# Five operand sums in three VectorE instructions, and score sums in other slots, in a fused attention and gated FFN kernel

## The chip, the cores and the metric

The kernel runs on one core of one Trainium2 chip. The metric is the device time of one execution in microseconds; lower is better. The kernel before took 802.4 us (median of three runs, 801.87 to 802.45).

## The reference

Cross-covariance attention over channels, then a gated feed-forward layer. Sizes: B = 4 batches, N = 6016 rows, C = 256 channels, 1536 hidden units.

```python
qn = q / (norm(q, axis=1) + 1e-6);  kn = k / (norm(k, axis=1) + 1e-6)
s = kn.transpose(0, 2, 1) @ qn / tau          # [B, 256, 256]
a = exp(s - max);  a /= a.sum(-1) + 1e-9
x = (v @ a).reshape(B * N, C)
out = (sigmoid(x @ w_gate) * (x @ w_val)) @ w_out
```

## The kernel before

Each batch has its attention matrix folded into the two FFN weights (`gh`), so that the main loop multiplies v directly with them. The main loop runs over 4 batches of 12 chunks; a chunk is four tiles of 128 rows (three in the last chunk of a batch). A chunk has 12 slots, one for each block of 128 hidden units. In slot f, `glu` makes the gate product (`ps_gate`, two matmuls of 512 columns) and the value product (`ps_val`, two more) on TensorE, ScalarE takes tanh of the first into `g_sb`, and VectorE multiplies (g_sb + 1) by `ps_val` into `hT[:, f]` (L682). The PSUM tiles `ps_gate` and `ps_val` have two buffers each, `g_sb` has three.

The output product of the chunk before (`out_work`, `product`) fills the slots: it is a Strassen-like scheme in which a 2 by 2 block product takes seven block products in place of eight. Its left operands are blocks of hT or sums of blocks (`sums`, made by `a_sum`, L704, on VectorE), its right operands are blocks of w_out or sums of them (`w_sums`, made once by `sum_w_out` on GpSimd, L228). A chunk's product is 84 matmuls of 128 columns, seven per slot. `part` and `whole` copy the results on ScalarE and add them on GpSimd (L759, L760, L775, L776), in float32 in SBUF.

The instructions of an engine run in the order in which the program writes them (a manual schedule). Slot by slot that is: `glu`; then an operand sum for the second half of the chunk before (`NEXT_SLOTS`); then the share of output matmuls (`run_work`); then an operand sum for the first half of this chunk (`OWN_SLOTS`); then the side work due in this slot (`side_work`). Side work prepares the next batch: it loads q and k, squares and accumulates them, makes the scores, and then the folded weights.

For the third and fourth batches the scores too are made in the seven-product form. The rows come in six groups of eight tiles, 16 slots apart; `s0` is the slot at which a group begins, counted from the start of the batch, and its place in a chunk is s0 % 12: 0, 4, 8, 0, 4, 8. `score_sums` makes sums of q and k blocks: number 0 at L351, number 2 at L359, numbers 3 and 4 at L364, all on VectorE; number 1 is made by DMA. `score_work` gives the score matmuls, which `queue_scores` puts in a queue and `run_scores` takes out evenly over the slots. `score_out` copies the two PSUM banks of scores at the end of the batch's scores, and `norms_mm` puts the norms into the second bank's free region.

All matmuls but the transposes at the start have the line L129, that of the helper `mm`.

Of the kernel before, what the change touches and what calls it, by code (L numbers as in the profile page):

```python
# [10 lines left out]
BF16 = mybir.dt.bfloat16  # L11
INT32 = mybir.dt.int32
ACT = mybir.ActivationFunctionType
ALU = mybir.AluOpType
PSUM = bass.MemoryType.PSUM


A_SUMS = (
    ((0, 1), ALU.subtract, (1, 1)),
    ((0, 0), ALU.add, (1, 1)),  # L20
    ((0, 0), ALU.add, (0, 1)),
    ((1, 0), ALU.add, (1, 1)),
    ((1, 0), ALU.subtract, (0, 0)),
)
B_SUMS = (
    ((1, 0), ALU.subtract, (0, 0)),
    ((0, 1), ALU.subtract, (1, 1)),
    ((1, 0), ALU.add, (1, 1)),
    ((0, 0), ALU.add, (1, 1)),
    ((0, 0), ALU.add, (0, 1)),  # L30
)

PRODUCTS = {
    "z1": (0, 1, 3),
    "y1": (1, (0, 0), 1),
    "x1": (2, (1, 1), 0),
    "x2": (2, 3, (0, 0)),
    "y2": (1, 2, (1, 1)),  # L40
    "z2": (0, 0, 2),
    "v2": (3, 4, 4),
}
ORDER = (
# [3 lines left out]
)  # L48
NEXT_SLOTS = {1: 1, 3: 3, 4: 2, 5: 0, 6: 4}
OWN_SLOTS = {7: 1, 8: 3, 9: 2, 10: 0, 11: 4}  # L50


@with_exitstack
def kernel(
# [20 lines left out]
    nc = tc.nc  # L75
    P = nc.NUM_PARTITIONS
# [9 lines left out]
    FC = DFF // P  # L86
# [3 lines left out]
    CH = TPC * P  # L90
# [73 lines left out]
    t0, nt = groups0[0]  # L164
# [39 lines left out]
    for f0, nf in pieces:  # L204
        if f0 + nf == DFF:
            load_v(0, 1)
        for w, src in enumerate((moe_w_gate, moe_w_val)):
            nc.gpsimd.dma_start(
                out=w_sb[w][f0 // FG][:, :, ds(f0 % FG, nf)],
# [3 lines left out]
    w_sums = consts.tile([P, len(B_SUMS), FC // 2, P], BF16)  # L213
    w_f32 = {}

    for n in range(FC // TPC):
        w_f32[n] = f32pool.tile([P, TPC, C], FP32, tag="f32", name="w_f32")
        nc.gpsimd.dma_start(
            out=w_f32[n], in_=moe_w_out.rearrange("(t p) c -> p t c", p=P)[:, n * TPC : (n + 1) * TPC, :]
# [5 lines left out]
    def sum_w_out(m, n):  # L225
        (k0, c0), op, (k1, c1) = B_SUMS[m]
        w = w_f32[n]
        nc.gpsimd.tensor_tensor(  # L228
            out=w_sums[:, m, n * 2 : (n + 1) * 2, :],
            in0=w[:, k0::2, ds(c0 * P, P)],  # L230
            in1=w[:, k1::2, ds(c1 * P, P)],
            op=op,
        )


    st = {}
# [454 lines left out]
    sums = {}  # L691

    def a_sum(b, ci, g, m):

        nt = groups[ci][1]
        half = nt // 2
        hT = hts[b, ci]
        if (b, ci, g) not in sums:
            sums[b, ci, g] = spool.tile(
                [P, len(A_SUMS), FC // 4, CH // 2], BF16, tag=f"s{g}", name="sums", bufs=2 - g  # L700
            )
        (r0, k0), op, (r1, k1) = A_SUMS[m]
        f0, f1 = g * (FC // 2), (g + 1) * (FC // 2)
        nc.vector.tensor_tensor(  # L704
            out=sums[b, ci, g][:, m, :, : half * P],
            in0=hT[:, f0 + k0 : f1 : 2, ds(r0 * half * P, half * P)],
            in1=hT[:, f0 + k1 : f1 : 2, ds(r1 * half * P, half * P)],
            op=op,
        )

    ffn = {}
    stores = []
# [91 lines left out]
    def run_work(work, share):  # L804

        upto = sum(w[0] for w in work) * share
        done = 0
        while work and done < upto:
            cost, fn, *args = work.pop(0)
            fn(*args)  # L810
            done += cost

    def store():
        while stores:
            b, ci = stores.pop(0)
            t0, nt = groups[ci]
            nc.sync.dma_start(out=out_rows[b][:, t0 : t0 + nt, :], in_=ffn.pop((b, ci))[:, :nt, :])
# [43 lines left out]
    for g, (t0, nt) in enumerate(groups0):  # L861
# [11 lines left out]
        while adds:  # L873
            w, last_sq = adds.pop()
# [55 lines left out]
    def side_work(b):  # L930


        side = {}

        def at(slot, fn, *a):
            side.setdefault(divmod(slot, FC), []).append((fn, a))

        for ci in range(NCH):
            nb, nci = (b, ci + 1) if ci + 1 < NCH else (b + 1, 0)
            lb, lci = (b, ci + 2) if ci + 2 < NCH else (b + 1, ci + 2 - NCH)  # L940
            if nb < B:
                at(ci * FC + 2, transpose_v, nb, nci)
            if lb < B:
                at(ci * FC + (10 if (b, ci) == (0, 0) else 0), load_v, lb, lci)
            if (b, ci) == (0, 0):
                for i in range(FC // TPC):
                    at(8, copy_w_out, i)
                for n, m in enumerate((1, 0, 3, 2, 4)):
                    for i in range(FC // TPC):
                        at(11 + 2 * n, sum_w_out, m, i)  # L950
        n = b + 1
        if n == B:
            return side
        first, last = (14 if b == 0 else 0), 8 * FC
        wide = [(t, min(2 * TPC, NT - t)) for t in range(0, NT, 2 * TPC)]
        at(first, acc_start, n)
        for g, (t0, nt) in enumerate(groups if b == 0 else []):
            s0 = first + g * (last - first) // NCH
            at(max(FC - 3, s0 - 12), load_qk, n, t0, nt)
            for u in range(nt):  # L960
                at(first + (t0 + u) * (last - first) // NT, score, n, t0, u)
            for w in range(2):
                at(s0 + 1 + 4 * w, narrow_square, n, g, w)
                slot = s0 + 3 + 4 * w
                at(slot + 2 if w == 0 and slot % FC == 8 else slot, narrow_add, n, g, w)
        step = (last - first) / len(wide)
        for g, (t0, nt) in enumerate(wide if b else []):
            s0 = first + int(g * step)
            halves = [(0, nt - TPC), (TPC, TPC)]
            if s0 >= 24:  # L970
                at(s0 - 24, load_qk, n, t0, nt)
            for i in range(4):
                at(s0 + 3 * i, acc_square, n, t0, 1 - i // 2, halves, i % 2)
            for w in range(2):
                at(s0 + 11 - 6 * w, acc_add, n, t0, w, halves)
            for m in (0, 2, 3, 4):
                at(s0 + 3 * max(0, m - 1), score_sums, n, t0, m, halves)
            ahead = 0 if g == 0 else 5
            at(s0 + 1 - ahead, score_sums, n, t0, 1, halves)
            at(s0 + 6 - ahead, score_sum_q, n, t0, halves)  # L980
            end = first + int((g + 1) * step) + 3
            at(s0 + 3, queue_scores, n, t0, halves)
            for slot in range(s0 + 3, end):
                at(slot, run_scores, s0 + 3, end, slot)
        if n + 1 < B:
            for g, (t0, nt) in enumerate(wide[:2]):
                at(NCH * FC - 24 + 16 * g, load_qk, n + 1, t0, nt)
        s0 = 8 * FC + 2
        if b == 0:
            at(s0, acc_fold, n, 0, (2, 1))  # L990
            at(s0 + 1, acc_fold, n, 1, (2, 1))
            at(s0 + 3, norms_mm, n)
            at(s0 + 4, root_seed, n)
            at(s0 + 4, root_steps, n)
            at(s0 + 10, norms_inv, n)
            at(s0 + 11, spread_both, n)
            at(s0 + 13, read_row, n)
        else:
            at(s0 - 3, acc_fold, n, 1, (4,))
            at(s0 - 2, acc_fold, n, 1, (2, 1))  # L1000
            at(s0, acc_fold, n, 0, (4,))
            at(s0 + 2, acc_fold, n, 0, (2, 1))
            at(s0 + 5, score_out, n, 0)
            at(s0 + 6, norms_mm, n)
            at(s0 + 7, score_out, n, 1)
            at(s0 + 7, root_seed, n)
            at(s0 + 7, root_steps, n)
            at(s0 + 12, norms_inv, n)
            at(s0 + 12, spread_both, n)
            at(s0 + 14, read_row, n)  # L1010
            at(s0 + 14, score_blocks, n)
        at(s0 + 22, scale_x, n, 0)
        at(s0 + 24, scale_x, n, 1)
        at(s0 + 25, exps, n, 0)
        at(s0 + 26, exps, n, 1)
        at(s0 + 28, all_sums, n)
        at(s0 + 28, gh_tiles, n)
        for i, piece in enumerate(gh_order):
            slot = s0 + 29 + 2 * i
            if slot < NCH * FC:  # L1020
                at(slot, gh, n, piece, *((pss, "s"), (psm, "m"))[i % 2])
            else:
                spill.setdefault((n, *divmod(slot - NCH * FC, FC)), []).append((gh, (n, piece, psm, "m")))
        return side
# [12 lines left out]
    for b in range(B):  # L1037
        side = side_work(b)
        for ci in range(NCH):
            final = (b, ci) == (B - 1, NCH - 1)  # L1040
            for f in range(FC):
                mid = gh_mid.get(f) if (b, ci) == (0, 0) else None
                glu(b, ci, f, None if mid is None else (lambda: gh_pieces(mid)))
                if prev is not None:
                    if f == 4:
                        store()
                    if f + final in NEXT_SLOTS and prev != (0, 0):
                        a_sum(*prev, 1, NEXT_SLOTS[f + final])
                    run_work(work, 1 / max(1, FC - final - f))
                if f in OWN_SLOTS and not final and (b, ci) != (0, 0):  # L1050
                    a_sum(b, ci, 0, OWN_SLOTS[f])
                for fn, a in spill.get((b, ci, f), []) + side.get((ci, f), []):
# [45 lines left out]
```

## Time and profile before

| engine | busy us of 799.6 | share |
|---|---|---|
| TensorE matmuls (PE) | 779.7 | 98% |
| VectorE (DVE) | 713.9 | 89% |
| ScalarE (ACT) | 525.6 | 66% |
| GpSimd (POOL) | 398.9 | 50% |

The span of the profiled execution, 799.6 us, is a little shorter than the time of a run. An instruction's busy time reaches from its start to its end as recorded, so where the next one starts before the end of the one before, single durations add up to more than the engine's time; the start of the next one is what shows the pace. In the rows of groups the columns are the line, engine, operation and tiles with shapes, the count, then busy time and mean ns of one, then the engine's idle time just before them and what ended it.

### The profile page before, as it was taken

To read this page: it belongs to the slowest core of one execution; us is meant where nothing else is said; L and a number is where in the kernel's file an instruction comes from. 1 tells how busy PE (TensorE), PEld (TensorE's weight loads), DVE (VectorE), ACT (ScalarE), POOL (GpSimd) and SP (SyncE) were. 2 spreads that over 40 slices of the span, in tenths; PEclk is the share of its full clock that TensorE was granted. 3 is DMA by queue.
4 is the path that set the end of the run, shared out by engine and by line. 5 is a ranking of instruction groups with operands and counts; after the bars stand their busy time and mean duration, and the time that the engine had idled before them with its cause. 6 is when DMAs were issued, how large, how long until landed. Compare 5 with 4: busy or idle time off the path is not lost.

```text
span 799.6 us, 18217 instructions
## 1 busy us (share of the span) xinstructions
PE 779.7 (98%) x6875; PEld 497.6 (62%) x6875; DVE 713.9 (89%) x1228; ACT 525.6 (66%) x891; POOL 398.9 (50%) x618
## 2 busy tenths in 40 slices
PE   3899999999999999999999999999999999999998
PEld 2556666666666666666666666666666566666666
DVE  5768999999979999999988999999998898998996
ACT  3666777766667767676667777666666565665664
POOL 3564545446453566565743565565744244444433
PEclk9999999999999999999999999999999999999999
DMA  9997758432777899862577699977234323423302
GB/s 214 198 199 133 131 96 139 93 67 54 135 143 140 170 174 200 171 114 54 115 137 146 132 163 186 174 147 139 56 66 84 67 56 80 74 60 72 82 27 74
DMA packets 82776, 95.16 MB, mean 119 GB/s; under 512 B 52512, under 2 KB 58528, under 8 KB 82688
## 3 DMA queue, kind: packets, MB, share of 16 engines
q0 software_dynamic: 25616, 55.85, 39.5%
q1 hardware_dynamic: 56496, 37.30, 21.2%
q8 instruction: 53, 0.87, 0.4%
q10 hardware_dynamic: 576, 0.85, 0.3%
q14 instruction: 35, 0.29, 0.1%
HBM read 79.04 MB, written 24.64 MB: 130 GB/s over the span
## 4 chain that ended last, share of the span: by engine, by line
PE 94%; DMA 4%; DVE 1%; issue 0%; ACT 0%; POOL 0%; DVEq 0%; POOLq 0%
PE ps_gate L129 30%; PE ps_val L129 30%; PE ps_o L129 27%; DMA qk_sb<-in_k_dram 4%; PE ps_s L129 4%; PE ps_gh L129 3%; DVE hT L682 0%; DVE sums L704 0%; DVE qs L364 0%; PE ps_end L129 0%; PE ps_n L129 0%; DVE x_sb L543 0%; PE ps_r L129 0%; ACT e_sb L561 0%; POOL qk_sb L148 0%
## 5 line engine op out<-in xcount | busy, mean ns | idle before, releaser
L681 ACT ACTIVATE g_sb<-ps_gate 128x512 f32<-128x512 f32 (+1 forms) x576 | 337.9, 589 | 224.7 <-PE ps_gate L129 212.3
L682 DVE SCALAR_TENSOR_TENSOR hT<-g_sb,ps_val 128x512 bf16<-128x512 f32 (+1 forms) x576 | 385.3, 670 | 67.1 <-ACT g_sb L681 52.3
L129 PE MATMUL ps_val<-vT,gh_H 128*128 128x512 bf16 (+1 forms) x1152 | 337.5, 375 | 0.5 <-DVE hT L682 0.5
L129 PE MATMUL ps_gate<-vT,gh_G 128*128 128x512 bf16 (+1 forms) x1152 | 337.6, 375 | 0.0
L704 DVE TENSOR_TENSOR sums<-hT 128x768 bf16<-128x768 bf16 (+1 forms) x460 | 283.4, 616 | 0.0
L129 PEld LDWEIGHTS <-sums 128*128 128x128 bf16 x2670 | 182.9, 98 | 82.2 <-DVE sums L704 0.4
L129 PEld LDWEIGHTS <-gh_H 128*128 128x128 bf16 x1152 | 112.7, 98 | 131.5 <-issue 1.2
L775 POOL TENSOR_TENSOR out_sb<-out_sb,m_sb 128x256 f32<-128x256 f32 x89 | 78.8, 885 | 186.1 <-ACT out_sb L765 163.0
L129 PE MATMUL ps_o<-w_sums,sums 128*128 128x128 bf16 x1602 | 154.4, 219 | 0.0
L129 PEld LDWEIGHTS <-hT 128*128 128x128 bf16 x1200 | 88.3, 98 | 46.8
L759 POOL TENSOR_TENSOR m_sb<-m_sb 128x128 f32<-128x128 f32 x89 | 44.9, 504 | 127.1 <-ACT m_sb L758 126.7
L129 PEld LDWEIGHTS <-gh_G 128*128 128x128 bf16 x1152 | 92.5, 98 | 12.2 <-DVE gh_G L629 0.3
L129 PE MATMUL ps_o<-w_out_sb,sums 128*128 128x128 bf16 x1068 | 96.2, 219 | 0.0
L129 PE MATMUL ps_o<-w_sums,hT 128*128 128x128 bf16 x1068 | 95.5, 219 | 0.0
L776 POOL TENSOR_TENSOR out_sb<-out_sb 128x256 f32<-128x256 f32 x89 | 76.6, 861 | 7.0
L760 POOL TENSOR_TENSOR m_sb<-m_sb 128x128 f32<-128x128 f32 x89 | 56.6, 636 | 7.0
L765 ACT COPY out_sb<-ps_o 128x512 f32<-128x512 f32 x89 | 52.2, 586 | 11.4 <-PE ps_o L129 8.9
L129 PE MATMUL ps_s<-qk_sb 128*128 128x256 bf16 (+1 forms) x194 | 34.1, 292 | 15.7 <-DMA qk_sb<-in_k_dram 8.6
L758 ACT COPY m_sb<-ps_o 128x384 f32<-128x384 f32 x89 | 42.6, 479 | 3.7 <-PE ps_o L129 1.1
L257 ACT ACTIVATE sq<-qk_sb 128x1024 bf16<-128x1024 bf16 (+3 forms) x36 | 35.6, 1009 | 12.0 <-DMA qk_sb<-in_k_dram 11.9
L297 ACT ACTIVATE sq<-qk_sb 128x1024 bf16<-128x1024 bf16 (+1 forms) x40 | 41.2, 1031 | 0.0
L129 PEld LDWEIGHTS <-qk_sb 128*128 128x128 bf16 x286 | 26.7, 102 | 21.7 <-issue 10.9
(102 smaller groups left out, 448.0 us busy)
## 6 DMA issues: line engine op xcount, KB each, us to landing
out_dram<-out_sb SPq DMA_DIRECT2D x43, 512.0 KB, 3.4
v_sb<-in_v_dram POOLq DMA_DIRECT2D x44, 256.0 KB, 5.4
acc<-sq POOLq DMA_DIRECT2D x16, 512.0 KB, 7.0
qk_sb<-in_q_dram POOLq DMA_DIRECT2D x14, 512.0 KB, 10.3
qk_sb<-in_k_dram POOLq DMA_DIRECT2D x14, 512.0 KB, 8.2
qs<-qk_sb POOLq DMA_DIRECT2D x20, 256.0 KB, 5.5
qk_sb<-in_q_dram POOLq DMA_DIRECT2D x15, 256.0 KB, 4.6
qk_sb<-in_k_dram POOLq DMA_DIRECT2D x15, 256.0 KB, 5.6
```

Source lines behind the costliest of these rows:

```text
L129: nc.tensor.matmul(out, lhsT=lhsT, rhs=rhs, start=start, stop=stop, **kw)
L257: nc.scalar.activation(out=sq[:, :nt, :], in_=src[:, :nt, :], func=ACT.Square)
L297: nc.scalar.activation(out=s["sq", w][:, u0 : u0 + n, :], in_=src[:, u0 : u0 + n, :], func=ACT.Square)
L681: nc.scalar.activation(out=g_sb[:, :n], in_=ps_gate[:, :n], func=ACT.Tanh, scale=0.5)
L682: nc.vector.scalar_tensor_tensor(out=hts[b, ci][:, f, :n], in0=g_sb[:, :n], scalar=1.0, in1=ps_val[:, :n], op0=ALU.add, op1=ALU.mult,)
L704: nc.vector.tensor_tensor(out=sums[b, ci, g][:, m, :, : half * P], in0=hT[:, f0 + k0 : f1 : 2, ds(r0 * half * P, half * P)], in1=hT[:, f0 ...
L758: nc.scalar.copy(m, states[p]["ps"][:, : 3 * P].rearrange("p (n c) -> p n c", c=P))
L759: nc.gpsimd.tensor_tensor(out=m[:, 1, :], in0=m[:, 1, :], in1=m[:, 2, :], op=ALU.add)
L760: nc.gpsimd.tensor_tensor(out=m[:, 2, :], in0=m[:, 1, :], in1=m[:, 0, :], op=ALU.add)
L765: nc.scalar.copy(o[:, p : p + half + 1 : half, :], states[p]["ps"].rearrange("p (t c) -> p t c", c=C),)
L775: add(out=ends, in0=ends, in1=states[p]["m"][:, 1:3, :], op=ALU.add)
L776: add(out=ends, in0=ends, in1=mids, op=ALU.subtract)
```

## The change

It does two things.

The first is on the operand sums of the output product. Five VectorE instructions for each half chunk, each of 768 elements per partition, become three: one of 768 and two that make two sums each, 1536 elements. For that the five sums are put in another order, and one of them, block (1, 0) minus block (0, 0), turns into its negative. To make up for it, one of the weight sums is multiplied by -1 once at the start. The product is the same sum of products. The sums, which were made in slots 7 to 11 and then 1, 3, 4, 5, 6, are now made in slots 7, 9, 11 and 1, 3, 5.

The second is on the score sums of the third and fourth batches. They are placed by a table (`SCORE_SLOTS`) that depends on where in a chunk the group begins, so that most fall into slots without operand sums; their products are queued five slots later (s0 + 8 in place of s0 + 3) and end five slots later; and the copies of the two score banks change places, the second bank first.

```diff
-A_SUMS = (
-    ((0, 1), ALU.subtract, (1, 1)),
-    ((0, 0), ALU.add, (1, 1)),
-    ((0, 0), ALU.add, (0, 1)),
-    ((1, 0), ALU.add, (1, 1)),
-    ((1, 0), ALU.subtract, (0, 0)),
-)
+A_STEPS = {0: (0, 1), 1: (1, 2), 2: (3, 2)}
...
-NEXT_SLOTS = {1: 1, 3: 3, 4: 2, 5: 0, 6: 4}
-OWN_SLOTS = {7: 1, 8: 3, 9: 2, 10: 0, 11: 4}
+NEXT_SLOTS = {1: 0, 3: 1, 5: 2}
+
+SCORE_SLOTS = {0: (0, 2, 12, 14), 4: (2, 8, 10, 13), 8: (4, 6, 9, 12)}
+OWN_SLOTS = {7: 0, 9: 1, 11: 2}
...
+        nc.gpsimd.tensor_tensor(out=out, in0=in0, in1=in1, op=op)
+        if m == 4:
+            nc.gpsimd.tensor_scalar(out=out, in0=out, scalar1=-1.0, scalar2=None, op0=ALU.mult)
...
-        (r0, k0), op, (r1, k1) = A_SUMS[m]
         f0, f1 = g * (FC // 2), (g + 1) * (FC // 2)
-        nc.vector.tensor_tensor(
-            out=sums[b, ci, g][:, m, :, : half * P],
-            in0=hT[:, f0 + k0 : f1 : 2, ds(r0 * half * P, half * P)],
-            in1=hT[:, f0 + k1 : f1 : 2, ds(r1 * half * P, half * P)],
-            op=op,
-        )
+        n = half * P
+        first, count = A_STEPS[m]
+        out = sums[b, ci, g][:, first : first + count, :, :n].rearrange("p m j n -> p j m n")
+        x = hT[:, f0:f1, : 2 * n].rearrange("p (j k) (r n) -> p j k r n", k=2, r=2)
+        if m == 0:
+            nc.vector.tensor_tensor(out=out[:, :, 0], in0=x[:, :, 0, 0], in1=x[:, :, 1, 1], op=ALU.add)
+        elif m == 1:
+            nc.vector.tensor_tensor(out=out, in0=x[:, :, 0], in1=x[:, :, 1], op=ALU.add)
+        else:
+            nc.vector.tensor_tensor(out=out, in0=x[:, :, :, 0], in1=x[:, :, :, 1], op=ALU.subtract)
...
-            for m in (0, 2, 3, 4):
-                at(s0 + 3 * max(0, m - 1), score_sums, n, t0, m, halves)
+            for m, slot in zip((0, 2, 3, 4), SCORE_SLOTS[s0 % FC]):
+                at(s0 + slot, score_sums, n, t0, m, halves)
...
-            end = first + int((g + 1) * step) + 3
-            at(s0 + 3, queue_scores, n, t0, halves)
-            for slot in range(s0 + 3, end):
-                at(slot, run_scores, s0 + 3, end, slot)
+            end = first + int((g + 1) * step) + 8
+            at(s0 + 8, queue_scores, n, t0, halves)
+            for slot in range(s0 + 8, end):
+                at(slot, run_scores, s0 + 8, end, slot)
...
-            at(s0 + 5, score_out, n, 0)
+            at(s0 + 5, score_out, n, 1)
             at(s0 + 6, norms_mm, n)
-            at(s0 + 7, score_out, n, 1)
+            at(s0 + 7, score_out, n, 0)
```

More of the change, by code (lines that the diff above doesn't have):

```diff
@@ L35 @@
 PRODUCTS = {
-    "z1": (0, 1, 3),
+    "z1": (0, 0, 3),
     "y1": (1, (0, 0), 1),
     "x1": (2, (1, 1), 0),
[L39 to L42, printed above, removed]
+    "x2": (2, 2, (0, 0)),
+    "y2": (1, 1, (1, 1)),
+    "z2": (0, 4, 2),
+    "v2": (3, 3, 4),
 }
@@ L227, in sum_w_out @@
         w = w_f32[n]
[L228 to L231, printed above, removed]
-            op=op,
-        )
+        out = w_sums[:, m, n * 2 : (n + 1) * 2, :]
+        in0, in1 = w[:, k0::2, ds(c0 * P, P)], w[:, k1::2, ds(c1 * P, P)]
+        nc.gpsimd.tensor_tensor(out=out, in0=in0, in1=in1, op=op)
+        if m == 4:
+            nc.gpsimd.tensor_scalar(out=out, in0=out, scalar1=-1.0, scalar2=None, op0=ALU.mult)
     st = {}
@@ L699, in a_sum @@
             sums[b, ci, g] = spool.tile(
-                [P, len(A_SUMS), FC // 4, CH // 2], BF16, tag=f"s{g}", name="sums", bufs=2 - g
+                [P, 5, FC // 4, CH // 2], BF16, tag=f"s{g}", name="sums", bufs=2 - g
             )
-        (r0, k0), op, (r1, k1) = A_SUMS[m]
         f0, f1 = g * (FC // 2), (g + 1) * (FC // 2)
-        nc.vector.tensor_tensor(
-            out=sums[b, ci, g][:, m, :, : half * P],
-            in0=hT[:, f0 + k0 : f1 : 2, ds(r0 * half * P, half * P)],
-            in1=hT[:, f0 + k1 : f1 : 2, ds(r1 * half * P, half * P)],
-            op=op,
-        )
+        n = half * P
[8 more added lines that the diff above has]
+            nc.vector.tensor_tensor(out=out, in0=x[:, :, :, 0], in1=x[:, :, :, 1], op=ALU.subtract)
     ffn = {}
```

## The prediction

> **What bounds the kernel now.** I read the page's head and its part 1 first, for the engine that is nearly always busy; then the chain that ended last, for whether that engine also sets the end; then the windows, for where it pauses; then the timeline, for what one pause is made of.
>
> ```profile
> span 799.6 us, 18217 instructions
> PE 779.7 (98%) x6875; PEld 497.6 (62%) x6875; DVE 713.9 (89%) x1228; ACT 525.6 (66%) x891; POOL 398.9 (50%) x618
> ...
> PE 94%; DMA 4%; DVE 1%; issue 0%; ACT 0%; POOL 0%; DVEq 0%; POOLq 0%
> ...
> L682 DVE SCALAR_TENSOR_TENSOR hT<-g_sb,ps_val 128x512 bf16<-128x512 f32 (+1 forms) x576 | 385.3, 670 | 67.1 <-ACT g_sb L681 52.3
> ...
> L704 DVE TENSOR_TENSOR sums<-hT 128x768 bf16<-128x768 bf16 (+1 forms) x460 | 283.4, 616 | 0.0
> ```
>
> TensorE is busy 779.7 of 799.6 us and carries 94% of the chain. VectorE is busy 89%, but only 1% of the chain is its own. The change works on VectorE (the L704 row and a few score sums). So what counts is how much TensorE waits for VectorE. The windows of 17 us say when TensorE pauses at all:
>
> ```profile
> 17.00:34.00 17.00, 11.56 (x95) 7.62 (x92) 13.93 (x24) 10.36 (x13) 7.48 (x13) 0.90 1.12 204
> 34.00:51.00 17.00, 16.27 (x94) 8.40 (x95) 12.92 (x24) 12.02 (x23) 9.03 (x13) 1.00 1.05 208
> 51.00:68.00 17.00, 17.00 (x108) 10.45 (x107) 10.63 (x18) 11.33 (x19) 15.30 (x24) 1.00 1.03 171
> ...
> 493.00:510.00 17.00, 16.66 (x158) 10.65 (x156) 15.89 (x25) 11.66 (x21) 12.55 (x19) 1.00 1.04 161
> 510.00:527.00 17.00, 16.79 (x160) 10.84 (x158) 16.75 (x28) 12.54 (x21) 8.69 (x13) 1.00 0.87 192
> ...
> 782.00:799.00 17.00, 14.75 (x165) 11.65 (x162) 9.83 (x20) 7.01 (x15) 6.00 (x10) 1.00 0.25 87
> ```
>
> The columns are the window, its length, then busy time of PE, weight loads, VectorE, ScalarE and GpSimd, and the granted clock. From 51 us to 782 us every window shows PE 17.00, but for two, which lack 0.34 and 0.21 us. The other idle time is the input phase up to 51 us and the last stores. The busy number hides short pauses, since the ends of matmuls are modelled; starts are safer. This is the timeline around the first pause:
>
> ```profile
> 498.51 0.59 PE L129 MATMUL ps_gate<-vT,gh_G 128*128 128x512 bf16 x2
> 498.94 0.59 PE L129 MATMUL ps_val<-vT,gh_H 128*128 128x512 bf16 x2
> 499.37 0.55 PE L129 MATMUL ps_o<-w_out_sb,sums 128*128 128x128 bf16 x7
> 499.76 0.28 PE L129 MATMUL ps_s<-qs 128*128 128x128 bf16 x2
> ...
> 501.24 0.59 PE L129 MATMUL ps_gate<-vT,gh_G 128*128 128x512 bf16 x2
> 502.09 0.59 PE L129 MATMUL ps_val<-vT,gh_H 128*128 128x512 bf16 x2 [0.25 <-DVE hT L682]
> ```
> ```profile
> 499.63 1.81 DVE L704 TENSOR_TENSOR sums<-hT 128x768 bf16<-128x768 bf16 x1
> 501.36 0.67 DVE L682 SCALAR_TENSOR_TENSOR hT<-g_sb,ps_val 128x512 bf16<-128x512 f32 x1
> ```
>
> Two 512-column matmuls start every 0.43 us, 0.215 each; seven 128-column ones take 0.39, 0.056 each. After 501.24 the next pair starts after 0.85 instead of 0.43: 0.42 lost. In the same way 0.25 is lost at 502.85 and 0.37 at 521.07 (a sum of q and k that took 1.85). These three, 1.04 us, with a few hundredths elsewhere, are all that TensorE loses to VectorE in the whole kernel: 1.1 us.
>
> **What the Trainium skill says.** "TensorE: Matmul & The Clock Gate", section "Wait — 56ns, not 53.3ns?", gives 55.6 and 215.7 ns from start to start for 128 and 512 columns on a warm array. The trace has 56 and 215, so TensorE is at its rate and only fewer matmuls, or fewer pauses, could shorten the middle. "VectorE: DVE Perf Modes", section "Mode 2×_1P", lets a two-input op take two elements a cycle where all operands are 16-bit with unit step. The trace agrees: 768 columns have a median of 550 ns and 1024 columns (L359, undisturbed) 682, thus 0.52 ns a column. "SBUF — State Buffer", section "SBUF: two separate sides", says that VectorE with two SBUF inputs and GpSimd exclude each other for a whole instruction. The trace agrees: the 1.81 us sum above lies over a GpSimd sum of 1.03 us.
>
> **The change, part by part.**
>
> 1. Matmuls: same number, shapes and operands per product; only the indices of the sums and a sign differ. Cost 0.
>
> 2. Five sums become three instructions. The elements stay at 5x768 per group. The old form is 550 ns, and 0.47 us from start to start in the timeline. The new pair of sums has 1536 columns: 550 + 768x0.52 = 950 ns, 0.87 from start to start. Per chunk (two groups): before 10x0.47 = 4.7, after 2x0.47 + 4x0.87 = 4.4 us. So about 0.3 us of a chunk of 16 us is freed, some 12 us in 46 chunks; as busy time, where the overlap of neighbours counts twice, 184x0.15 = 28 us, so L704's 283 become some 255 and VectorE's 714 some 687. Fewer instructions also meet fewer GpSimd sums. None of this is on the chain. Bounds for the new form, which no row shows: 0.95 us if rows of 256 contiguous values keep two elements a cycle (L359 reads rows of 128 in the same way and does), 1.65 us at one a cycle (768 more at 1.04 each, twice 0.52, would be added). I take 0.95.
>
> 3. Longer blocks. Behind each new sum the next hT waits, and behind that ps_val, which has two buffers. Slack: a slot without scores is 4x0.215 + 7x0.056 = 1.25 us, with them about 1.35. A free hT starts about 1.26 after its slot's first gate matmul (490.54 to 491.80) and ends 0.69 later, at 1.95; the ps_val that reuses its buffer starts at 2x1.35 + 0.43 = 3.13. Slack 1.2 us. A slot with hT (0.60) and a double sum (0.87) asks for 1.47, 0.12 over; the following slot has no sum and recovers that. A GpSimd wait of up to 1.26 (1.81 - 0.55) can just reach the slack.
>
> 4. Score sums (L351, L359, L364). They move mostly to even slots, where no operand sum is due. But of six groups per batch those that start at slot 4 or 8 of a chunk put one into slot 5: 0.60 + 0.87 + 0.60 = 2.07 in one slot, 0.72 late, which leaves 0.5 us. This occurs four times in the preparation of each of two batches. With a GpSimd wait of 1.26 each would stall 0.8 us, at most 6 us; with the usual small waits (616 mean against 550 median, 0.07) none. I take a fifth to a quarter of the eight at about 0.4 us: 0.8 us. Set against this, the crowded run of slots 7 to 11, where before each slot had a sum, is thinned out, and with it both pauses of the trace.
>
> 5. Score products start five slots later, all five inputs are ready a slot or more ahead, and the copies of the two banks change places: same matmuls in the same phase. The late end (slot 103) is before the first bank is copied at 105. Cost 0, hidden behind matmuls of the next chunks.
>
> 6. Three more GpSimd instructions turn the sign of one weight sum, once, near 65 us. The nearest row is L228, 764 ns for 256 columns: 2.3 us at most. Behind them only loads for later chunks and sums of m_sb wait, and the trace has GpSimd idle for 8.45 us before 74.77. Cost 0.
>
> Sum: 802.4 - 1.1 (pauses that go) + 0.8 (new ones) = 802.1; I say 802.0.
>
> **Rivals.**
>
> A, likeliest: paced by TensorE, 801.3 (all pauses gone) to 803.2 (some new ones). 80%.
>
> B, a new wait in place of the old: the double sums with a score sum or a GpSimd wait on top stall ps_val often. If all eight crowded slots cost 0.8 (6.4) and the old 1.1 goes, 802.4 + 5.3 = 807.7; if half do, 804.5. Slower. For it: both pauses in the trace are of this kind, and VectorE has few free slots. Against it: only three pauses in some 550 slots although sums of up to 1.85 occurred. 12%.
>
> C, the new access pattern loses the doubled rate: 4 double sums at 1.6 from start to start instead of 0.87, 2.9 us a chunk. VectorE would need 12x0.60 + 2x0.47 + 4x1.6 = 14.5 a chunk; with about 1 us of waits 15.5 against TensorE's 12x1.25 = 15.1, and in the 16 chunks with score sums (three each, 1.8) 17.3 against 16.2: 16x1.1 + 30x0.4 = 30 us, 832. Slower. Against it: L359 and L364. 3%.
>
> D, faster by more than the visible pauses: all that VectorE holds up in the trace is 1.1 us, so 800.5 would need gains in the input phase or at the end, where the change has nothing. 5%, for what a measurement may shift.
>
> **How the numbers follow.** The predicted time is A's, 802.0. The range is 801.0 to 804.2: below, all pauses gone and a little of spread (the three runs of before differ by 0.6); above, nearly to half of B. It leaves out the rest of B, C and most of D. 0.2% is 1.6 us: under 800.8 is D, 5%; over 804.0 is nearly all of B and C, 15%; the rest 80%.
>
> **What would show it.** The group of sums over hT has 276 instructions, the long ones near 950 ns, and VectorE's busy time falls by 20 to 35 us: step 2. A mean near 1.65 us would be C. The waits list has TensorE behind hT with under 1 us in all: steps 3 and 4; several us there, with ps_val after a slot 5 in windows from 200 to 560 us, would be B. Matmuls keep 0.056 and 0.215 us between starts: step 1. The prediction is wrong if TensorE pauses where it does not now, or if an unchanged stream of matmuls runs at another pace.

## The result, and the profile after

The changed kernel takes 804.94 us (median of six runs, 803.58 to 805.44); the kernel before, in six runs, 802.21 (801.67 to 803.05). The ratio is 1.0032, with a 95% interval of 1.0019 to 1.0045: slower, and above the range of 801.0 to 804.2. This is the direction of rival B. The execution with the profile took 805.34.

First the page of the changed kernel: span, part 1, the engines in the chain, and the rows of hT and of the operand sums, which are now L705 (the single sum), L707 and L709 (the double sums). Lines have moved by two or three: mm is L127, hT is L679.

```profile
span 803.6 us, 18036 instructions
PE 781.9 (97%) x6875; PEld 497.6 (62%) x6875; DVE 692.2 (86%) x1044; ACT 525.4 (65%) x891; POOL 437.7 (54%) x621
...
PE 93%; DMA 4%; DVE 2%; issue 1%; ACT 0%; POOL 0%; DVEq 0%; ACTq 0%; POOLq 0%
...
L679 DVE SCALAR_TENSOR_TENSOR hT<-g_sb,ps_val 128x512 bf16<-128x512 f32 (+1 forms) x576 | 382.9, 670 | 93.0 <-ACT g_sb L678 76.6
...
L707 DVE TENSOR_TENSOR sums<-hT 128x1536 bf16<-128x1536 bf16 (+1 forms) x92 | 103.7, 1127 | 0.0
...
L709 DVE TENSOR_TENSOR sums<-hT 128x1536 bf16<-128x1536 bf16 (+1 forms) x92 | 92.6, 1007 | 0.0
...
L705 DVE TENSOR_TENSOR sums<-hT 128x768 bf16<-128x768 bf16 (+1 forms) x92 | 50.7, 551 | 0.0
```

VectorE did what the change is for: 184 instructions fewer, and busy time down from 713.9 to 692.2 us. Yet its share of the chain rose from 1% to 2%, and the span by 4.0 us. GpSimd rose too, from 398.9 to 437.7, with three small instructions more: instructions of the same shape last longer, which I read as waiting that is recorded as part of their duration. Two of its rows (before: 885 and 636 ns):

```profile
L775 POOL TENSOR_TENSOR out_sb<-out_sb,m_sb 128x256 f32<-128x256 f32 x89 | 88.8, 998 | 174.9 <-ACT out_sb L765 153.5
...
L760 POOL TENSOR_TENSOR m_sb<-m_sb 128x128 f32<-128x128 f32 x89 | 78.0, 876 | 7.0
```

The windows of 17 us, in the columns of the prediction, say where TensorE now pauses. These are three of those with most of it. The list of waits has the wait of ps_val for hT as before, five times as long in sum; in its second line weight loads, which run ahead of the matmuls, wait for operand sums:

```profile
272.00:289.00 17.00, 16.22 (x154) 10.30 (x152) 15.05 (x21) 12.28 (x20) 9.61 (x15) 1.00 0.91 177
...
476.00:493.00 17.00, 15.94 (x151) 10.10 (x149) 16.38 (x24) 11.32 (x19) 12.98 (x16) 1.00 0.98 182
510.00:527.00 17.00, 16.66 (x159) 10.67 (x157) 15.81 (x21) 12.50 (x21) 11.07 (x14) 1.00 0.86 181
```
```profile
PE ps_val L127 <- DVE hT L679: 2.4, 5, 0.8
PEld L127 <- DVE sums L705: 1.9, 6, 0.4
```

All three lie where the scores of the third and fourth batches are made. By starts of matmuls, taking what each loses beyond its 0.056 or 0.216 us where that is over 0.06 us, TensorE pauses for 5.0 us between 45 and 790 us, against 1.1 us before. I call this sum "the pauses" below; records of matmuls that a trace lacks are left out of it. The difference of 3.9 us is the difference of the spans, 4.0. There are 18 pauses: in 16 of them, 4.7 us, ps_val waits for hT, and in two of 0.15 us a product waits for its double sum itself.

The largest pauses are two of 0.94 us, 194 us apart, at the same place of the two batches. The timeline of the changed kernel there, first TensorE, then VectorE, GpSimd and ScalarE:

```profile
282.47 0.59 PE L127 MATMUL ps_gate<-vT,gh_G 128*128 128x512 bf16 x2
283.84 0.59 PE L127 MATMUL ps_val<-vT,gh_H 128*128 128x512 bf16 x2 [0.78 <-DVE hT L679]
```
```profile
280.52 0.69 DVE L679 SCALAR_TENSOR_TENSOR hT<-g_sb,ps_val 128x512 bf16<-128x512 f32 x1 [0.65 <-ACT g_sb L678]
281.12 2.07 DVE L348 TENSOR_TENSOR qs<-qk_sb 128x1024 bf16<-128x1024 bf16 x1
283.11 0.67 DVE L679 SCALAR_TENSOR_TENSOR hT<-g_sb,ps_val 128x512 bf16<-128x512 f32 x1
```
```profile
280.99 0.88 POOL L366 DMA_DIRECT2D qs<-qk_sb  x1 [4.60 <-DMA qs<-qk_sb]
281.59 1.04 POOL L775 TENSOR_TENSOR out_sb<-out_sb,m_sb 128x256 f32<-128x256 f32 x1
282.71 1.06 POOL L776 TENSOR_TENSOR out_sb<-out_sb 128x256 f32<-128x256 f32 x1
```
```profile
278.94 1.06 ACT L294 ACTIVATE sq<-qk_sb 128x1024 bf16<-128x1024 bf16 x1
279.90 1.08 ACT L678 ACTIVATE g_sb<-ps_gate 128x512 f32<-128x512 f32 x2
```

The score sum of 0.68 us took 2.07. It started while GpSimd was issuing the accumulating DMA of `score_sum_q` (L366), with an output add (L775) queued behind. It ended 0.68 after 282.51, so it could not begin in earnest before the add was nearly over. hT came late by that, and ps_val had no free buffer.

The hold-up of 1.39 us is not all of it. The hT at 283.11 belongs to the slot whose gate matmuls start at 279.74; a free one would have come 1.26 us after that, at 281.00, so it was 2.1 us late, and less the slack of 1.2 us that is the pause of 0.94. The other 0.7 us come from the score sum's own 0.60 and from ScalarE: its square L294 stood in front of the tanh that the hT at 280.52 needed, and that hT was 0.9 us late. By this sum the hold-up with ScalarE on time would have cost next to nothing (0.60 + 0.60 + 1.39 of work in a slot of 1.37, so 1.2 late); that is an estimate, and no run tests it.

Behind a double sum no such help is needed. At 312.1 and 522.66 pauses of 0.45 and 0.27 us follow double sums that were held up in the same way, though the hT in front was on time. The first lies over the accumulating DMA of L305:

```profile
309.82 2.29 DVE L707 TENSOR_TENSOR sums<-hT 128x1536 bf16<-128x1536 bf16 x1
```
```profile
309.64 0.89 POOL L305 DMA_DIRECT2D acc<-sq  x1
310.25 1.04 POOL L775 TENSOR_TENSOR out_sb<-out_sb,m_sb 128x256 f32<-128x256 f32 x1
```

### The profile page after: what moved, and what is told of

Its sections match the earlier page's. It is cut to its first block, busy times and chain, and to the rows that moved or that the text cites. A ratio compares the mean times of both kernels' runs of the same rounds, so it can differ in the third digit from the quotient of the medians.

```text
span 803.6 us, 18036 instructions
## 1 busy us (share of the span) xinstructions
PE 781.9 (97%) x6875; PEld 497.6 (62%) x6875; DVE 692.2 (86%) x1044; ACT 525.4 (65%) x891; POOL 437.7 (54%) x621
## 4 chain that ended last, share of the span: by engine, by line
PE 93%; DMA 4%; DVE 2%; issue 1%; ACT 0%; POOL 0%; DVEq 0%; ACTq 0%; POOLq 0%
PE ps_val L127 30%; PE ps_gate L127 30%; PE ps_o L127 27%; DMA qk_sb<-in_k_dram 4%; PE ps_s L127 4%; PE ps_gh L127 3%; DVE hT L679 1%; DVE sums L707 0%; ACT g_sb L678 0%; PE ps_end L127 0%; ACT sq L294 0%; PE ps_n L127 0%; DVE acc L312 0%; DVE acc L331 0%; DVE x_sb L540 0%
## 5 line engine op out<-in xcount | busy, mean ns | idle before, releaser
L679 DVE SCALAR_TENSOR_TENSOR hT<-g_sb,ps_val 128x512 bf16<-128x512 f32 (+1 forms) x576 | 382.9, 670 | 93.0 <-ACT g_sb L678 76.6
L127 PE MATMUL ps_val<-vT,gh_H 128*128 128x512 bf16 (+1 forms) x1152 | 337.5, 375 | 2.5 <-DVE hT L679 2.4
L127 PE MATMUL ps_gate<-vT,gh_G 128*128 128x512 bf16 (+1 forms) x1152 | 337.6, 375 | 0.0
L127 PEld LDWEIGHTS <-sums 128*128 128x128 bf16 x2670 | 182.6, 98 | 82.8 <-DVE sums L705 1.9
L127 PEld LDWEIGHTS <-gh_H 128*128 128x128 bf16 x1152 | 112.6, 98 | 135.4 <-issue 6.6
L775 POOL TENSOR_TENSOR out_sb<-out_sb,m_sb 128x256 f32<-128x256 f32 x89 | 88.8, 998 | 174.9 <-ACT out_sb L765 153.5
L127 PE MATMUL ps_o<-w_sums,sums 128*128 128x128 bf16 x1602 | 154.7, 219 | 0.0
L127 PEld LDWEIGHTS <-hT 128*128 128x128 bf16 x1200 | 88.2, 98 | 46.9
L707 DVE TENSOR_TENSOR sums<-hT 128x1536 bf16<-128x1536 bf16 (+1 forms) x92 | 103.7, 1127 | 0.0
L759 POOL TENSOR_TENSOR m_sb<-m_sb 128x128 f32<-128x128 f32 x89 | 49.8, 559 | 97.9 <-ACT m_sb L758 97.4
L127 PEld LDWEIGHTS <-gh_G 128*128 128x128 bf16 x1152 | 92.8, 98 | 12.7 <-DVE gh_G L626 0.3
L127 PE MATMUL ps_o<-w_out_sb,sums 128*128 128x128 bf16 x1068 | 96.2, 219 | 0.0
L127 PE MATMUL ps_o<-w_sums,hT 128*128 128x128 bf16 x1068 | 95.5, 219 | 0.0
L709 DVE TENSOR_TENSOR sums<-hT 128x1536 bf16<-128x1536 bf16 (+1 forms) x92 | 92.6, 1007 | 0.0
L760 POOL TENSOR_TENSOR m_sb<-m_sb 128x128 f32<-128x128 f32 x89 | 78.0, 876 | 7.0
L776 POOL TENSOR_TENSOR out_sb<-out_sb 128x256 f32<-128x256 f32 x89 | 77.4, 870 | 7.0
L705 DVE TENSOR_TENSOR sums<-hT 128x768 bf16<-128x768 bf16 (+1 forms) x92 | 50.7, 551 | 0.0
L127 PE MATMUL ps_s<-qk_sb 128*128 128x256 bf16 (+1 forms) x194 | 34.9, 298 | 15.4 <-DMA qk_sb<-in_k_dram 8.8
```

The source lines that it names most:

```text
L127: nc.tensor.matmul(out, lhsT=lhsT, rhs=rhs, start=start, stop=stop, **kw)
L679: nc.vector.scalar_tensor_tensor(out=hts[b, ci][:, f, :n], in0=g_sb[:, :n], scalar=1.0, in1=ps_val[:, :n], op0=ALU.add, op1=ALU.mult,)
L705: nc.vector.tensor_tensor(out=out[:, :, 0], in0=x[:, :, 0, 0], in1=x[:, :, 1, 1], op=ALU.add)
L707: nc.vector.tensor_tensor(out=out, in0=x[:, :, 0], in1=x[:, :, 1], op=ALU.add)
L709: nc.vector.tensor_tensor(out=out, in0=x[:, :, :, 0], in1=x[:, :, :, 1], op=ALU.subtract)
L759: nc.gpsimd.tensor_tensor(out=m[:, 1, :], in0=m[:, 1, :], in1=m[:, 2, :], op=ALU.add)
```

## The experiments

Theory 1: a VectorE instruction with two SBUF inputs that meets a GpSimd add is held up, and double sums and moved score sums now overrun the slack of the PSUM buffers when that happens. Theory 2: the double sums are too long by themselves. Theory 3: the moved score sums are the cost, not the operand sums. All experiments were timed beside the kernel before. The times are medians of many executions; the pauses are those of one execution, the profiled one.

| kernel | us | before, same chip | ratio (95%) | pauses in its profile, us |
|---|---|---|---|---|
| changed | 804.94 | 802.21 | 1.0032 (1.0019-1.0045) | 5.0 |
| changed, again | 804.92 | 801.28 | 1.0045 (1.0032-1.0059) | 2.5 |
| sums only | 803.96 | 801.76 | 1.0022 (1.0013-1.0031) | 2.5 |
| scores only | 803.71 | 801.76 | 1.0026 (1.0018-1.0034) | 3.6 |
| no GpSimd adds | 801.23 | 801.76 | 0.9991 (0.9979-1.0004) | 0.9 |
| pairs split | 811.65 | 801.76 | 1.0116 (1.0101-1.0131) | 10.3 |
| sums in quiet slots | 802.37 | 801.64 | 1.0011 (1.0002-1.0020) | 2.1 |
| DMA later | 803.14 | 801.64 | 1.0034 (1.0018-1.0050) | 2.3 |
| DMA later, again | 802.43 | 801.28 | 1.0015 (1.0006-1.0024) | 1.9 |
| quiet and later | 802.57 | 801.64 | 1.0015 (0.9998-1.0032) | 1.7 |
| quiet start | 800.53 | 801.28 | 0.9996 (0.9985-1.0007) | 0.5 |
| quiet start, again | 800.65 | 801.50 | 0.9993 (0.9986-1.0000) | 0.6 |

**Sums only.** The score part goes back to what it was:

```diff
-            for m, slot in zip((0, 2, 3, 4), SCORE_SLOTS[s0 % FC]):
-                at(s0 + slot, score_sums, n, t0, m, halves)
+            for m in (0, 2, 3, 4):
+                at(s0 + 3 * max(0, m - 1), score_sums, n, t0, m, halves)
...
-            end = first + int((g + 1) * step) + 8
+            end = first + int((g + 1) * step) + 3
...
-            at(s0 + 5, score_out, n, 1)
+            at(s0 + 5, score_out, n, 0)
...
```

> The changed kernel with the score sums, score queue and score copies as before: the three-instruction operand sums alone. Theory 1 (a VectorE instruction of two SBUF inputs that meets a GpSimd add, and is twice as long, overruns the 1.2 us slack of the PSUM buffers): most of the new pauses stay, those behind L348 go; pauses of TensorE between 45 and 790 us of about 2 to 3.5 us in all, +1 to +2.5 us over before. Theory 3 (the moved score sums are the cost): pauses near 1 us, the time of before within 0.5 us.

2.2 us over before, pauses 2.5 us; the pauses of 0.94 us behind L348 are not there. Theory 3 falls as a whole explanation. But 1.5 of the 2.5 us are of another kind than the theories say: at 368, 371, 477, 483, 561 and 564 us a matmul starts right after the sum that it reads has ended (the largest, 0.48 us at 477, after an operand sum that took 1.81 us over L366 and L775). So late sums cost not only through hT and the PSUM buffers, but also directly.

**Scores only.** The kernel before, with SCORE_SLOTS, the later queue and the exchanged copies, but five operand sums in the old slots.

> The kernel before with the score part of the change alone: five operand sums in their old slots, score sums and score queue in the new ones. Theory 1: the two pauses of 0.94 us behind the score sum L348, which meets the issue of an accumulating DMA and the output add behind it, stay or move, the others do not exist: 1 to 3 us of pauses, 0 to +2 us over before. Theory 3: +2.5 us, the whole of the loss. If the moved slots only help: time of before or 1 us less.

2.0 us over before by the medians, at the upper end of what was expected. The pauses repeat in both batches: 0.4 us after the first score sum of a group had taken 1.52, 0.35 after another of 1.21, and 0.52 each in two crowds at the end of the scores, which also lie over GpSimd's adds. So each half costs about two parts in a thousand alone, and together they cost 0.32% and 0.45% in the two measurements. Within these intervals the two halves may simply add up, but they need not: the moved score sums were placed for slots that the new operand sums leave empty, and here the old ones still sit in slots 4, 6, 8 and 10.

**No GpSimd adds.** From the changed kernel, L759, L760, L775 and L776 are taken out; the block products are copied but not combined, so the output lacks these sums:

```diff
-            nc.gpsimd.tensor_tensor(out=m[:, 1, :], in0=m[:, 1, :], in1=m[:, 2, :], op=ALU.add)
-            nc.gpsimd.tensor_tensor(out=m[:, 2, :], in0=m[:, 1, :], in1=m[:, 0, :], op=ALU.add)
...
-            add(out=ends, in0=ends, in1=states[p]["m"][:, 1:3, :], op=ALU.add)
-            add(out=ends, in0=ends, in1=mids, op=ALU.subtract)
```

> The changed kernel without the four GpSimd adds that combine the block products (L759, L760, L775, L776 are left out, so the output lacks these sums); everything on the other engines is the same. Theory 1: double sums last 0.95 us without exception except against DMA issues, pauses fall from 5 us to under 1 us, about 801 us. Theory 2 (the double sums are too long by themselves, whatever GpSimd does): pauses stay near 4 to 5 us, 804 to 805 us.

This decides between theories 1 and 2. The double sums are as long and in the same slots, and the loss is gone. These are the double sums in that run:

```profile
L709 DVE TENSOR_TENSOR sums<-hT 128x1536 bf16<-128x1536 bf16 (+1 forms) x92 | 85.6, 931 | 0.0
L707 DVE TENSOR_TENSOR sums<-hT 128x1536 bf16<-128x1536 bf16 (+1 forms) x92 | 85.0, 924 | 0.0
```

1127 and 1007 ns became 924 and 931. What is left of the pauses, 0.9 us, is one event at 498 us; there hT waits 2.56 us for ScalarE, not for a sum. The work that was taken out also lay on GpSimd's own queue, so the run alone doesn't say that it is the meeting and not, say, a later DMA. The kernels with quiet slots below keep the adds and so speak to that.

**Pairs split.** The slots of the change, but two sums of 768 back to back for each double one:

```diff
-            nc.vector.tensor_tensor(out=out, in0=x[:, :, 0], in1=x[:, :, 1], op=ALU.add)
+            for r in range(2):
+                nc.vector.tensor_tensor(out=out[:, :, r], in0=x[:, :, 0, r], in1=x[:, :, 1, r], op=ALU.add)
...
```

> The changed kernel with each double sum written as two sums of 768, back to back in the same slot. Theory 1: the same elements block hT for the same time, and two instructions can be held twice, but GpSimd can come in between: pauses of 4 to 7 us, time within 1.5 us of the changed kernel. If the length of one instruction is what matters (GpSimd kept out for 0.95 us and then blocking for longer), pauses fall to 1 to 2 us and the time to within 1 us of before.

Worse than both expectations: 9.9 us over before, pauses of 10.3 us and 12 waits of ps_val for hT, 4.8 us in the list of waits. The timeline shows one such place, first VectorE, then GpSimd. Of the pair the first sum starts ahead of the add and takes 0.55 us; the second takes 1.08 over L777, and the next VectorE instruction, L331, 1.21 in place of 0.69 over L778:

```profile
136.32 1.55 DVE L711 TENSOR_TENSOR sums<-hT 128x768 bf16<-128x768 bf16 x2
137.80 1.21 DVE L331 TENSOR_TENSOR acc<-acc,sq 128x1024 bf16<-128x1024 bf16 x1
```
```profile
136.58 0.88 POOL L777 TENSOR_TENSOR out_sb<-out_sb,m_sb 128x256 f32<-128x256 f32 x1 [1.34 <-ACT out_sb L767]
137.53 0.92 POOL L778 TENSOR_TENSOR out_sb<-out_sb 128x256 f32<-128x256 f32 x1
```

Over the whole trace 197 of the 460 operand sums took over 0.1 us longer than alone, against 98 of 276 in the changed kernel, where they lie in the same slots, and 112 of 460 in the kernel before. So to make two sums in one instruction is worth having: in the same slots it is about 7 us better. That leaves the slots as what lost it.

**Sums in quiet slots.** To find these, take for each operand sum its duration less 550 ns (950 for a double one) and average by slot, the slot being that of the last hT in front of it. In the kernel before, slots 3, 5, 8, 9 and 11 have 0.23, 0.12, 0.19, 0.16 and 0.09 us of it; 1, 4, 6, 7 and 10 have 0.03 or less. In the changed kernel 3, 5, 9 and 11, just where the double sums went, have 0.23, 0.12, 0.17 and 0.06; 1 and 7, where the single ones went, 0.02 or less. The starts of GpSimd's adds lie in the same slots: L759 and L760 in 3 and 5, L775 and L776 in 8, 9, 11 and 0, since the products end there. With the sums-only kernel as its base:

```diff
-NEXT_SLOTS = {1: 0, 3: 1, 5: 2}
+NEXT_SLOTS = {1: 0, 2: 1, 4: 2}
...
-OWN_SLOTS = {7: 0, 9: 1, 11: 2}
+OWN_SLOTS = {6: 1, 7: 0, 10: 2}
```

> Three-instruction operand sums alone (as in the first experiment: score part as before), but in slots in which the trace of the changed kernel has hardly a GpSimd add: 1, 2, 4 and 6, 7, 10 in place of 1, 3, 5 and 7, 9, 11. If the meetings with GpSimd adds are the cost: mean of the double sums falls from 1.0 to 1.1 us to about 0.97, pauses from 2.5 to about 1 us or less, time about 802, 1.5 to 2 us under the first experiment. If the length of the double sums or the crowding of slots is the cost: 804, pauses of 2.5 us or more.

802.37, 0.7 us over before where the sums-only kernel was 2.2 over. The two ratios were measured on different chips and their intervals overlap, so by the times alone the gain isn't shown. What is shown is that the sums are no longer held up: the double sums come down to 943 and 948 ns, from 1125 and 992 in the sums-only kernel. The pauses remain at 2.1 us, more than expected. The largest, 0.85 us, follows a meeting of a double sum (1.67 us) and a score sum (1.21) with GpSimd; two of 0.32 us, at the start of both batches, follow none.

**DMA later.** The changed kernel with the accumulating DMA of q at slot s0 + 8:

```diff
-            at(s0 + 6 - ahead, score_sum_q, n, t0, halves)
+            at(s0 + 8, score_sum_q, n, t0, halves)
```

> The changed kernel with one edit: the accumulating DMA for the q sum (score_sum_q) is issued at slot s0+8 of its group in place of s0+1, so that GpSimd does not sit waiting for the copy in front of it while output adds queue up behind. If the worst waits (2.1 to 2.3 us for an instruction of 0.68 or 0.95) come from a VectorE instruction that starts during such an issue with an add queued behind: the two pauses of 0.94 us and that of 0.27 go, pauses fall from 5.0 to about 3 us, time 1 to 2.5 us less than the changed kernel. If the issue of the DMA has no part in it: same pauses at other places, time within 0.5 us of the changed kernel.

> The accumulating DMA for the q sum at s0+8, once more, since its interval was wide. If the pauses carry the time: 2.3 us of pauses against some 5 of the changed kernel, so 2 to 3 us less than it on the same chip. If the time does not follow the pauses: within 0.5 us of it.

The three pauses behind L366 are gone in both profiles, and the pauses are 2.3 and 1.9 us. The first timing showed no gain: its ratio is that of the changed kernel, with a wide interval, since four of its 22 executions took 808.7 to 811.0 us, for which no trace gives a cause. Its profiled execution also started the main loop 1.9 us later than that of the changed kernel (the matmuls that come at 48.1 us there come at 50.0), in the input phase, where the edit does nothing. The second timing, on one chip with the changed kernel, has 802.43 against 804.92, with intervals that don't overlap. The run of the unedited changed kernel beside it:

> The changed kernel, unedited, once more, so that it stands beside the next two on one chip. Pauses of 4 to 6 us at the same places of the two batches (the first slots of the fourth chunk of a batch, 0.9 us each), ratio to before 1.002 to 1.0045. If the pauses fall elsewhere from run to run, no place of the program but chance makes them.

Its two pauses of 0.94 us did not come back: in this profile another score group was hit, at 330 us, with 0.44 and 0.25 us behind a double sum of 2.27 us that met L366 and L775. Pauses of 0.10 to 0.22 us did return at 110, 176, 273, 355, 466 and 548 us, each behind a double sum that met m_sb's adds. That profiled execution took 802.8 us, the least of its six. L366 and L775 lay over the score sum L348 here too, at 281 us, but it started 0.07 us after the issue in place of 0.13, and took its usual 0.69 us. So which group is hit differs from run to run, by a few hundredths of a microsecond at this place; L366 waits for another DMA to land (4.60 us in the lines above), so its start isn't fixed by the program. The meetings with the adds of m_sb came back at the same places.

**Quiet and later**, with score sums placed in the slots that double sums leave free:

```diff
-SCORE_SLOTS = {0: (0, 2, 12, 14), 4: (2, 8, 10, 13), 8: (4, 6, 9, 12)}
+SCORE_SLOTS = {0: (3, 5, 9, 12), 4: (1, 4, 5, 8), 8: (0, 3, 7, 9)}
```

> The changed kernel with both edits, and its score sums placed so that they do not share slots with the double sums in 1, 2, 4, 6, 7, 10 (in slots 0, 3, 5, 8, 9, 11 of a chunk). If GpSimd meetings are the cause of all of the loss: pauses under 1.1 us, time equal to before or up to 1 us less, 801 to 802. If something else in the change costs: 803 or more.

802.57, within its interval of before but not under it. Of the 1.7 us of pauses 1.4 are 0.44 and 0.27 us at the start of the scores of both batches, with no GpSimd add near. There is only a crowd on VectorE, in slots where TensorE has no score matmuls yet and so is faster:

```profile
239.42 0.55 DVE L709 TENSOR_TENSOR sums<-hT 128x768 bf16<-128x768 bf16 x1
239.89 0.68 DVE L679 SCALAR_TENSOR_TENSOR hT<-g_sb,ps_val 128x512 bf16<-128x512 f32 x1
240.49 0.75 DVE L626 TENSOR_SCALAR gh_H<-ps_gh,rrow 128x512 bf16<-128x512 f32 x1
241.15 0.68 DVE L356 TENSOR_TENSOR qs<-qk_sb 128x1024 bf16<-128x1024 bf16 x1
241.75 0.68 DVE L679 SCALAR_TENSOR_TENSOR hT<-g_sb,ps_val 128x512 bf16<-128x512 f32 x1
242.35 0.95 DVE L707 TENSOR_TENSOR sums<-hT 128x1536 bf16<-128x1536 bf16 x1
```

VectorE works here without a gap from 238.82 us on, and hT comes 1.86 us after the one in front of it (239.89 to 241.75), where TensorE takes 1.14 us for a slot. So length and crowding do count, at this one place; theory 2 is not nothing.

**Quiet start.** The same, with the first group's score sums moved off that crowd:

```diff
-            for m, slot in zip((0, 2, 3, 4), SCORE_SLOTS[s0 % FC]):
+            for m, slot in zip((0, 2, 3, 4), SCORE_SLOTS[s0 % FC] if g else (3, 9, 12, 13)):
```

> The version with quiet slots and the later DMA, with the score sums of a batch's first group at slots 3, 9, 12, 13 in place of 3, 5, 9, 12. If the pauses of 0.44 and 0.27 us at the start of both batches came from the crowd of hT, folded-weight stores, score sums and double sums there and not from GpSimd: they go, pauses of about 0.3 to 0.6 us in all, time 0.5 us under before at best. If not: 1.7 us as they were.

> The last version once more, since its interval (0.9985 to 1.0007) leaves open whether it is faster than before. By the pauses (0.5 us against 1.1) it can be 0.6 us faster, a ratio of 0.9993; by the medians of the last run 0.75 us. If the ratio comes out at 0.999 to 1.000 again, it equals before or is a little faster; if above 1.001, the last run was luck.

Of these pauses 0.1 us is left in each batch. The page of the second run shows what the merged sums bring when hardly anything meets them (before: 713.9 us and 398.9 us):

```profile
span 798.9 us, 18038 instructions
...
PE 779.9 (98%) x6875; PEld 497.9 (62%) x6875; DVE 665.8 (83%) x1044; ACT 525.4 (66%) x891; POOL 379.0 (47%) x621
```

The medians are 0.75 and 0.85 us under before, ratios 0.9996 and 0.9993. The first interval holds 1, the second ends at it. The version beats the changed kernel by 4.4 us on one chip (800.53 against 804.92), with all GpSimd adds in place. That, with the run without adds, is what shows the meetings with GpSimd as the main cause; how much of the 4.4 us is due to the quiet slots, to the later DMA and to the moved score sums isn't separated. Over the kernel before it is ahead by about what the pauses had room for (1.1 less 0.5), and no more can be claimed.

## Why the prediction was wrong

Its frame held. TensorE sets the pace, the matmuls kept their 0.056 and 0.215 us between starts, and nearly all that the change did to the time it did through pauses of ps_val behind hT. Step 1 was right. Step 2 was right in the unit: an undisturbed double sum takes 0.95 us, so rival C was rightly set aside (its bound of 1.65 us should be 1.75 by its own terms, 950 and 768 times 1.04 ns). VectorE's busy time fell by 22 us, within the 20 to 35 us that the prediction gave, but not for its reason: on the page an overlap of neighbours counts once, so the 28 us don't apply. By step 2's 0.3 us a chunk some 12 us come from the shorter work, and the rest fits what the operand sums lost by being held up, which fell from 36 to 28 us. Step 3's slack of 1.2 us is confirmed by the largest pause: 2.1 us late, 0.94 lost. Steps 5 and 6 showed nothing.

One reading was wrong too. Of the three pauses of before, that at 502.85 isn't "in the same way": there the next matmul, a score product, starts at 503.16, right after the score sum that it reads has ended (502.43 and 0.68). Sums can hold TensorE directly, as they do in the sums-only kernel.

The step that failed is the count of new pauses. "I take a fifth to a quarter of the eight at about 0.4 us: 0.8 us", from step 4, stood for all new pauses; step 3 put those outside the eight crowded slots at nothing. The profile has 18 pauses, 5.0 us together. The eight slots, where a double sum and a score sum share slot 5, were not far off: seven of them paused, 1.3 us in all. The other 3.8 us came where the prediction had nothing: 1.9 behind the score sum L348, 1.1 behind double sums in slots 9 and 11 that met a DMA issue with an add behind it, 0.8 in six small ones. Three things were wrong.

- Step 4 took slots without operand sums to be free, and looked for danger only where three VectorE instructions fall into one slot. The two worst pauses came behind a score sum with no operand sum in its slot. What mattered there was GpSimd's work in the slot, and a late ScalarE in front of it.
- Step 4 used the usual wait (0.07 us on average over all sums) although the old sums were spread over ten slots of a chunk, five of them quiet. The change put all four double sums of a chunk into 3, 5, 9 and 11, where before a sum lost 0.23, 0.12, 0.16 and 0.09 us, and none into a quiet one. The trace of before held these numbers.
- Step 3 gave the double sum 1.26 us of wait at worst and found that this "can just reach the slack". By its own numbers it passes it: the wait and the 0.12 us by which the slot is over make 1.38, against 1.2. Waits of 1.34 us (2.29 less 0.95) occurred.

The sentence "Fewer instructions also meet fewer GpSimd sums" was true: 98 held-up sums in place of 112, and 28 us lost in place of 36. Yet TensorE paused more. What counts is not the sum of the waits but whether one of them, on top of a longer instruction, passes the slack. The pauses of before were expected to go, and they did go at 501 and 521 us; others came elsewhere. Rival B named the mechanism and was given 12%. That its 804.5 is near the 804.94 measured is luck: it took half of the eight slots at 0.8 us, and the eight cost 1.3 us in all. Its argument against, that only three pauses existed in some 550 slots, counted a layout that the change was about to leave.

## What to carry to other kernels

Where one engine sets the pace and another stands behind it with a slack of about one slot, average busy time says little; tabulate by slot how much longer than alone an instruction takes, and put the long ones into the slots where that is near zero. Merging two instructions with two SBUF inputs into one halved the number held up by GpSimd here (98 against 197), and splitting them back cost 7 us, but the merged one should lie where GpSimd has little to do. A DMA issued by GpSimd that has to wait for another transfer lets its other work pile up behind it (L366 waited eight times in the changed kernel, 30.2 us in all); issue it when its input has long landed, if its result has time.

## What the runs showed of the hardware

A DMA issue on GpSimd does not by itself hold up a VectorE sum, with few exceptions. In the kernel before, 67 such sums started during an issue with no GpSimd add before their end, and none was longer by more than 0.01 us; in the changed kernel one of 44 was, by 0.35 us (at 313.23), which is not explained. But where an add came directly behind the issue, 7 of 12 in the changed kernel were held up. Five of them lost 0.94 to 1.39 us, that is until shortly before the end of the add, although by the record the add had not started when they did; the other two started together with the add and lost 0.3 us. A VectorE sum that started ahead of an add with no issue under way was not delayed: 46 in the changed kernel, none by more than 0.01 us. That VectorE with two SBUF inputs and GpSimd exclude each other is in the Trainium skill ("SBUF — State Buffer", "SBUF: two separate sides"), and the trace agrees: the second sum of the split pair above took 1.08 us in place of 0.55, over an add of 0.88. That an add reaches back over the issue in front of it is what I had not expected. Why it does so, and why it did not for 5 of the 12, is not shown here.
